# Cross-attention and gated FFN on one core: x of batches 2 to 7 transposed in 32 by 32 blocks on VectorE, scores on sixteen array tiles, a new order for batch 0 and for the periods

## Chip, core and metric

The kernel runs on one core of one Trainium2 chip. The metric is the device time of one execution in microseconds (us). Engines are named as the profile names them: PE is TensorE's matmul queue and PEld its weight loads, DVE is VectorE, ACT ScalarE, POOL GpSimd, SP SyncE, which issues nearly all DMAs.

## What is computed

Per batch (8) and head (8), 512 tokens of x (64 wide) and 32 states are read against each other in both directions; the result, 544 rows of 512 per batch, goes through an RMS norm and a gated FFN with 1536 hidden columns.

```python
B, H, S, Ns, D = (8, 8, 512, 32, 64)
scores = scale * np.matmul(x, state.transpose(0, 1, 3, 2))
a = np.exp(scores - max);  a /= a.sum(-1, keepdims=True) + 1e-09
xread = np.matmul(a, state)                  # tokens read the states
scores2 = scale * np.matmul(state, x.transpose(0, 1, 3, 2))
sread = np.matmul(softmax(scores2), x)       # states read the tokens
x = concatenate([xread, sread], axis=2)      # -> (B*544, 512)
xn = x / sqrt(mean(x * x) + 1e-06) * rms_g
out = (silu(xn @ w_gate) * (xn @ w_val)) @ w_out
```

The three weights come as 64-bit floats, x and state as 32-bit.

## The kernel before

All matmuls are 32-bit; one matmul leaves two MATMUL records in the trace, a transpose leaves one.

The work is a list of **streams**, Python generators whose every `yield` ends one step. Three letter strings, `ORDER`, `PERIOD` and `STATES` (lines 22 to 40), written out by a planner, say which stream takes its next step; within `tc.manual_schedule` they fix the order of the instructions on TensorE, VectorE and ScalarE, each of which takes its queue strictly in that order. GpSimd's and SyncE's queues are ordered by the framework.

- **Batch 0** (`ORDER`, lines 886 to 892). Streams e and d (lines 185 and 208) turn the 64-bit weights into 32-bit ones, 18 pieces of 128 by 1024, the first in two halves: three ScalarE and four VectorE instructions a piece. Meanwhile a (`tokens_read(0)`) and s (`states_read(0)`) do batch 0's attention, A and S batch 1's. v projects a pair of weight blocks onto the states (line 454), h are the hidden products (line 496), t and u their activation, p the output projection (line 694). z (`keep_awake`, line 845) are filler products on TensorE whose results nobody reads.
- **Batches 1 to 7** (`PERIOD`, lines 897 to 920): one period per batch. h, t, u form six pairs of hidden blocks with seven products each (`hidden_seven`, lines 590 to 685; TensorE line 600), 42 steps of h in all; p, c, k project with seven products (`project_seven`, from line 738; TensorE line 754), 14 steps of p. Within period b the streams a and s do the attention of batch b+1, w and v project weights onto states (line 454), x copies them out and lets GpSimd form sums.
- **The states' rows** of all batches come last (`STATES`, lines 921 to 929) in the same seven-product scheme at half width.

**Attention of a batch's tokens** (`tokens_read`, lines 267 to 362): the packed states are transposed on TensorE (272) and copied (275); x, loaded as four chunks of 128 tokens, is transposed on TensorE by 16 transposes (282) in four bursts, each copied by ScalarE (284). Eight products with 64 rows and 32 columns of weights and 512 moving columns (291) give the scores in two PSUM banks. VectorE transposes them in 32 by 32 blocks (302), ScalarE keeps a copy for the states' read (304); maximum, difference, exponential, sum and quotient follow (311 to 327), the transpose back (329), and the read (336: eight products in four row groups, four banks). Squares (343), their sums over four tiles (346), a product with ones (350), the root on GpSimd (254), its spread over the rows (261) and the scaling of `aT_s` (360) end it.

**The states' read** (`states_read`, lines 364 to 411) uses the kept scores: maximum, exponential, eight transposes (385), 32 products (397), one more transpose (408). Line 397 is the last reader of x's buffer; x has two buffers, so the load of batch b+2 can start once batch b's line 397 is done.

SBUF and PSUM come from tile pools: `aps` and `vps` have two PSUM banks each ("at" and "pv"), `fx` two, `fy` and `fz` one. Weights `w_m` have three buffers; each product of line 454 asks for the pair three further on (line 158).

Of the kernel before, what the change touches and what calls it, by code (L numbers as in the profile page):

```python
# [8 lines left out]
F32 = mybir.dt.float32  # L9
# [8 lines left out]
P = 128  # L18
# [4 lines left out]
    "aaaaaaaaddaaaaaaeaseeaasadsasszzzzzzzzzzzzzzssdsaaaasaeadesaeeazzsdasaaezzzzzzza"  # L23
    "deadaaaddeeazzzzsedaadszzzzzadaeedzzvvavdzzadeaAzzzzhdeeddtdAdAAhueheAeedtddphAe"
    "dvdvduvdphedeAedtdhApeehddeuAdddeAhdedvdtudvvpeAAAAdhdAAteAehuhpddephepdeAdAeApA"
    "dteedAAvvveAdpudAAephtdSdhAdphdeAueedhAdeAteudddeeSppAddAAdppAdAdevApvdveehhAdth"
    "AudhpdeddeedeAdteAupvdvdvphedAAtdShhutSAhpukSSSkkkwSwkpSkpwpSSckSScckkpcSwkkkwww"
    "w"
# [3 lines left out]
    "hthtvvhhtuxxhuhthuhththuuhtuuhhxxhhuvxutvhtthuuhuhthuuxhxhxuxtthuhuthhuthuxxhuta"  # L32
    "uahatuhtaxuuuhtauahuahhaahuttuhutauhhhtuuahuhuutauphuauupuauapacasapaaaapapaskaa"
    "aaksacccassppakckpaaackasaapakapaskaaaswpksksswsxxwxxpxcspcskx"
# [4 lines left out]
    "yhuhttyuhuhuuhuthhyuthythytuhuuhuhutuuhuuppcpkpcpukkcpkpkpc"  # L39
# [4 lines left out]
def kernel(  # L44
# [9 lines left out]
):  # L54

# [42 lines left out]
    rows = {}  # L98
    x_sb = {}
# [7 lines left out]

    def load_x(b, *queues):
        x_sb[b] = two.tile([P, NC, H * D], F32, name="x_b")
        for c in range(NC):  # L110
            (queues or (nc.sync,))[c % max(1, len(queues))].dma_start(
                out=x_sb[b][:, c].rearrange("p (h d) -> p h d", h=H),
                in_=x[b, :, P * c:P * c + P, :].rearrange("h p d -> p h d"))
# [153 lines left out]
    def tokens_read(b):  # L267
        xb, packed = x_sb[b], rows.pop(b)
        stT = two.tile([P, 4, Ns], F32, name="stT")
        stT_g[b] = two.tile([P, 4, Ns], F32, name="stT_g")  # L270
# [27 lines left out]
        eS = one.tile([P, 2, S // Ns, Ns], F32, name="eS", tag="eS")  # L298
        m1 = two.tile([P, 2, S // Ns], F32, name="m1")
        z1 = two.tile([P, 2, S // Ns], F32, name="z1")  # L300
# [5 lines left out]

        def along(t, e):
# [13 lines left out]
        for e in range(2):  # L321
            VE.reduce_sum(out=z1[:, e], in_=eS[:, e], axis=AXX)
# [22 lines left out]
        for i, j in ((0, 1), (2, 3), (0, 2)):  # L345
            VE.tensor_tensor(out=sq[:, i, :], in0=sq[:, i, :], in1=sq[:, j, :], op=ALU.add)
            yield
        sp = aps.tile([P, NC], F32, name="at")
# [241 lines left out]
    def hidden_seven(n, weights, tokens, silu, after=lambda mp: None):  # L590
# [67 lines left out]
        def sums():  # L658
            for mp, q in enumerate(pairs):
# [8 lines left out]
                for i, val in ((1, q["c"]), (0, q["x"][:, :, 0:half])):  # L668
# [290 lines left out]
```

## Time and profile before

| what | value |
|---|---|
| median of 3 runs | 800.66 us (800.29 to 801.45) |
| the profiled execution | 800.68 us, span of its instructions 798.9 us |
| TensorE matmul busy | 786.0 us (98%), 4902 records |
| VectorE busy | 515.0 us (64%), 786 instructions |
| ScalarE busy | 347.0 us (43%) |
| GpSimd busy | 179.0 us (22%) |
| DMA | 94.13 MB, 118 GB/s on average |
| chain that ended last | PE 93%, DVE 5% |
| one period, batches 1 to 6 (scores to scores) | 86.90 us |
| line 282 in all | 128 transposes, 0.273 us each as recorded |
| line 845 (filler) | 80 records, 11.2 to 38.2 us |

The span is cut by the program's own structure: batch 0 up to about 141 us, periods of 86.90 us, the states' rows from about 740 us. Times in the views are from the start of the span. A busy share says how full an engine is, not what waits for what; for that the timeline of one engine shows in brackets how long it was idle ahead of an instruction and what released it. A record's own duration contains its pipeline, so the cost of a matmul to the queue is read from start to start.

### The profile page before, as it was taken

The numbers are of one execution on the slowest core, as the hardware profiler recorded it, in microseconds if no ns is written. First come the engines' busy times: TensorE is split into PE (matmuls) and PEld (weight loads), VectorE is DVE, ScalarE is ACT, GpSimd is POOL, SyncE is SP. The second block draws the span as 40 slices with busy tenths as digits, with TensorE's granted clock in tenths as the row PEclk, the third lists the DMA queues.
The fourth block names the chain that finished last, engine by engine and source line by source line (L and its number), as shares of the span: only waits on it lengthen the run. The fifth ranks groups of instructions, "written<-read, shape, count | busy, mean of one in ns | idle before, by whom it ended". The sixth has DMA issues, their size and how long they took to land.

```text
span 798.9 us, 12273 instructions
## 1 busy us (share of the span) xinstructions
PE 786.0 (98%) x4902; PEld 605.2 (76%) x4902; DVE 515.0 (64%) x786; ACT 347.0 (43%) x572; POOL 179.0 (22%) x216
## 2 busy tenths in 40 slices
PE   6999999999999999999999999999999999999998
PEld 5643444788778887888778877888788877888996
DVE  4999996688347842786358833785278635881461
ACT  5998864553245323543255314532354324510320
POOL 0000003530154004510433015500451044400000
PEclk9999999999999999999999999999999999999999
DMA  9987746700182007400461018200540024101311
GB/s 285 262 289 287 263 159 186 264 23 14 34 273 106 1 24 218 185 1 16 127 240 44 4 34 283 107 1 14 193 163 2 14 109 181 66 4 43 113 54 28
DMA packets 61593, 94.13 MB, mean 118 GB/s; under 512 B 38752, under 2 KB 46432, under 8 KB 54624
## 3 DMA queue, kind: packets, MB, share of 16 engines
q1 hardware_dynamic: 59360, 92.75, 34.2%
q10 hardware_dynamic: 2176, 0.59, 0.3%
q8 instruction: 39, 0.64, 0.3%
q14 instruction: 18, 0.15, 0.1%
HBM read 78.12 MB, written 15.20 MB: 117 GB/s over the span
## 4 chain that ended last, share of the span: by engine, by line
PE 93%; DVE 5%; issue 0%; DMA 0%; ACT 0%; SPq 0%
PE f L600 37%; PE f L754 35%; PE f L694 5%; PE pv L496 3%; PE at L454 3%; PE pv L454 3%; PE at L282 2%; PE at L291 1%; DVE ex L232 1%; PE at L397 1%; PE at L336 1%; DVE raw L228 1%; PE at L350 1%; PE at L385 1%; DVE w_m L237 1%
## 5 line engine op out<-in xcount | busy, mean ns | idle before, releaser
L754 PE MATMUL f<-wo,hb 128*128 128x256 f32 x540 | 124.2, 382 | 0.4 <-ACT ot L791 0.2
L662 DVE TENSOR_TENSOR g<-g,f 128x512 f32<-128x512 f32 (+1 forms) x96 | 62.8, 654 | 90.1 <-PE f L600 86.6
L600 PE MATMUL f<-aT_s,v 128*128 128x256 f32 x504 | 119.5, 380 | 0.0
L754 PEld LDWEIGHTS f<-wo,hb 128*128 128x128 f32 x540 | 101.4, 190 | 20.1 <-ACT ot L791 6.9
L600 PEld LDWEIGHTS f<-aT_s,v 128*128 128x128 f32 x504 | 93.8, 190 | 17.3 <-issue 5.2
L254 POOL TENSOR_TENSOR ri<-ss,mhalf 128x4 f32<-128x4 f32 x8 | 9.2, 1156 | 361.8 <-DVE ss L354 361.8
L600 PE MATMUL f<-aT_t,vs 128*128 128x256 f32 x336 | 87.2, 382 | 0.0
L754 PE MATMUL f<-wt,hs 128*128 128x256 f32 x360 | 80.4, 379 | 0.0
L653 ACT ACTIVATE hb<-g 128x1024 f32<-128x1024 f32 (+1 forms) x48 | 48.2, 1004 | 63.0 <-DVE g L662 63.0
L754 PEld LDWEIGHTS f<-wt,hs 128*128 128x128 f32 x360 | 68.3, 190 | 9.5 <-issue 0.2
L791 ACT COPY ot<-f 128x256 f32<-128x256 f32 x60 | 21.5, 372 | 122.5 <-PE f L754 122.5
L600 PEld LDWEIGHTS f<-aT_t,vs 128*128 128x128 f32 x336 | 62.6, 190 | 15.1 <-issue 5.9
L665 DVE SCALAR_TENSOR_TENSOR hb<-hb,g 128x1024 f32<-128x1024 f32 x42 | 55.5, 1320 | 7.8 <-ACT hb L653 7.8
L651 ACT COPY g<-f 128x512 f32<-128x512 f32 (+1 forms) x48 | 26.9, 561 | 76.7 <-PE f L600 76.7
L483 POOL TENSOR_TENSOR vs<-v,vs 128x256 f32<-128x256 f32 x42 | 58.3, 1389 | 0.0
L480 POOL TENSOR_TENSOR vs<-v 128x256 f32<-128x256 f32 x42 | 30.5, 727 | 118.6 <-ACT v L465 118.6
L694 PE MATMUL f<-wo,hb 128*128 128x512 f32 x96 | 44.7, 600 | 0.0
L600 PE MATMUL f<-aT_t,v 128*128 128x256 f32 x168 | 43.9, 383 | 0.0
L496 PE MATMUL pv<-aT_s,v 128*128 128x512 f32 x96 | 43.6, 593 | 0.0
L600 PE MATMUL f<-aT_s,vs 128*128 128x256 f32 x168 | 43.1, 379 | 0.0
L754 PE MATMUL f<-wt,hb 128*128 128x256 f32 x180 | 42.6, 386 | 0.0
L754 PE MATMUL f<-wo,hs 128*128 128x256 f32 x180 | 41.6, 382 | 0.0
(131 smaller groups left out, 1263.4 us busy)
## 6 DMA issues: line engine op xcount, KB each, us to landing
w_m<-w_d SPq DMA_DIRECT2D x48, 1024.0 KB, 6.5
x_b<-in_x_dram SPq DMA_DIRECT2D x30, 256.0 KB, 4.6
out_dram<-ot SPq DMA_DIRECT2D x56, 128.0 KB, 1.8
raw<-in_moe_w_val_dram SPq DMA_DIRECT2D x6, 1024.0 KB, 5.1
raw<-in_moe_w_out_dram SPq DMA_DIRECT2D x6, 1024.0 KB, 7.6
w_d<-w_m SPq DMA_DIRECT2D x6, 1024.0 KB, 4.9
raw<-in_moe_w_gate_dram SPq DMA_DIRECT2D x5, 1024.0 KB, 6.4
raw<-in_moe_w_gate_dram SPq DMA_DIRECT2D x2, 512.0 KB, 4.8
```

The source lines that it names most:

```text
L454: TE.matmul(out=pv[e][Ns * j:Ns * j + Ns, :], lhsT=stT_g[b][D * e:D * e + D, j, :], rhs=w[D * e:D * e + D, j].rearrange("p m k f -> p (m k ...
L480: GE.tensor_tensor(out=vs[:, 0], in0=a21, in1=a22, op=ALU.add)
L483: GE.tensor_tensor(out=vs[:, 2], in0=a12, in1=vs[:, 1], op=ALU.subtract)
L496: TE.matmul(out=to[0], lhsT=lhs(i, k), rhs=r, start=(i == 0), stop=(i == len(rhs) - 1))
L600: TE.matmul(out=ps[:, i, 0:half], lhsT=l[:, i, :], rhs=r, start=(start and i == 0 and k == 0), stop=(k == len(lhs) - 1), skip_group_check= ...
L651: SE.copy(gates(q)[1], q["x"][:, :, 0:half])
L653: SE.activation(out=hb[:, 2 * mp:2 * mp + 2, 0:n].rearrange("p m (c t) -> p m c t", c=2), in_=q["g"][:, :, :, 0:half], func=ACTF.Silu if s ...
L662: VE.tensor_tensor(out=to, in0=to, in1=q[ps][:, :, 0:half], op=ALU.add)
L665: VE.scalar_tensor_tensor(out=h, in0=h, scalar=1.0, op0=ALU.add, op1=ALU.mult, in1=q["g"].rearrange("p m c t -> p m (c t)"))
L694: TE.matmul(out=banks[r], lhsT=hb[:, m, P * r:P * r + P], rhs=wo[:, m, :], start=(m == 0), stop=(m == NM - 1))
L754: TE.matmul(out=banks[name][:, r, :], lhsT=lhs(k)[:, P * r:P * r + P], rhs=rhs(k), start=(start and r == 0 and k == 0), stop=(k == HM - 1) ...
L791: SE.copy(to, banks[name][:, r, :])
```

## The change

**x and scores of batches 2 to 7.** x is loaded by sixteen DMAs of 32 partitions in place of four of 128, so that partition 32g+p of chunk c holds token 128g+32c+p. A new tile `fours` holds all eight heads' states four times, once in each group of 32 partitions, by four DMAs. `scores_of_blocks` transposes `fours` (one VectorE instruction of 128 by 512) and x (two of 128 by 1024) in 32 by 32 blocks; 64 products with 32 rows and 32 columns of weights and 128 moving columns form the scores in four PSUM banks, two of "at" and two of "pv", one for each row group. Their transposes, copies and transposes back are four of 256 columns in place of two of 512. The packed states are still transposed on TensorE, later, straight from PSUM into `stT_g`. Batches 0 and 1 keep the old way (`scores`).

**Batch 0.** Its squares are added by TensorE, sixteen products with ones accumulated in PSUM, in place of three VectorE sums and four products. `ORDER` is new: 31 filler steps in place of 40; batch 0's states' read, all 14 of whose steps stood ahead of the first h, comes late (ten of its steps before the last h, line 397's after it). `slot_sums(1)` moves from the opening of the late pools into the first step of w.

**Periods and states.** `PERIOD` is new: a's first VectorE steps stand after 15, 21 and 24 steps of h, its products of scores after 34; the products of line 336 stand after six steps of p (before: eight); the second pair of v stands after 21 steps of h (before: 15). In `STATES` one p stands ahead of the last h. In `hidden_seven` the first of the two sums of the later pairs comes one step earlier where the activation is Silu (the states' rows).

```diff
--- before.py
+++ after.py
@@ -20,23 +20,22 @@
 W_BUFS = 3
 
 ORDER = (
-    "aaaaaaaaddaaaaaaeaseeaasadsasszzzzzzzzzzzzzzssdsaaaasaeadesaeeazzsdasaaezzzzzzza"
-    "deadaaaddeeazzzzsedaadszzzzzadaeedzzvvavdzzadeaAzzzzhdeeddtdAdAAhueheAeedtddphAe"
-    "dvdvduvdphedeAedtdhApeehddeuAdddeAhdedvdtudvvpeAAAAdhdAAteAehuhpddephepdeAdAeApA"
-    "dteedAAvvveAdpudAAephtdSdhAdphdeAueedhAdeAteudddeeSppAddAAdppAdAdevApvdveehhAdth"
-    "AudhpdeddeedeAdteAupvdvdvphedAAtdShhutSAhpukSSSkkkwSwkpSkpwpSSckSScckkpcSwkkkwww"
-    "w"
+    "aaaaaaaaadaedeeaaaaaaaaaaeeaaaaaaeaeaaazzzzzzzzzzzzzzzzzzzzaeaaaeddddaddzzzzaadd"
+    "deedaaadzvdaeevddzzaeavdedzzzAzhdAeAdtheeheuhAdddAdpetAeduedevvdpvepAhdAedteddde"
+    "hAueheddApdddepvevhdddevdtdupeddeAeehAtshppAAdhduhdedddeeAveeApvdpvdstuededAddeh"
+    "htpddehetpuAddshpvdeuAsedvspAAAAApveshAhAsdtAdudedhedsehtAsAApupdeeAedAppddAdAAv"
+    "AedAvAdpAsvAhSSetdhuShAdhtukkAASwsSkwkkwSpSSSSkpcpSkwskkkckSwpcSSscskwwww"
 )
 
 PERIOD = (
-    "hthtvvhhtuxxhuhthuhththuuhtuuhhxxhhuvxutvhtthuuhuhthuuxhxhxuxtthuhuthhuthuxxhuta"
-    "uahatuhtaxuuuhtauahuahhaahuttuhutauhhhtuuahuhuutauphuauupuauapacasapaaaapapaskaa"
-    "aaksacccassppakckpaaackasaapakapaskaaaswpksksswsxxwxxpxcspcskx"
+    "hhtvvhthhxthxhuhuttuhhthtuuuhhuxuhhxuaxthuthtthuuhhxuutuhtvavhxxtuhxxhtuahuuhhhu"
+    "uxhttuhuhttxhuhhauuuhuthtuatahahtuuuhahhuupuutaauhaauuuuaaaaaaaaaaapapsccaapappa"
+    "ckapcsaukaaasaapacakpaaasksaskkckspsskpspkswwsxwppxxxxsxkscc"
 )
 
 STATES = (
     "hyyyyhthyytthhhuuhtuhththhytuuhuuhthuhhtthyuhyyutyhhhuuuttyuhhutyyhhthuhyhuhuttu"
-    "yhuhttyuhuhuuhuthhyuthythytuhuuhuhutuuhuuppcpkpcpukkcpkpkpc"
+    "yhuhttyuhuhuuhuthhyuthythytuhuuhuhutuuphuupcpkpcpukkcpkpkpc"
 )
 
 
@@ -96,6 +96,7 @@
 
 
     rows = {}
+    fours = {}
     x_sb = {}
 
     def load_state(b):
@@ -105,8 +106,22 @@
             src = state[b, 2 * j:2 * j + 2].rearrange("e n d -> n e d")
             nc.sync.dma_start(out=rows[b][Ns * j:Ns * j + Ns], in_=src)
 
+    def load_fours(b):
+
+        fours[b] = one.tile([P, H, D], F32, name="fours")
+        for g in range(4):
+            nc.sync.dma_start(out=fours[b][Ns * g:Ns * g + Ns],
+                              in_=state[b].rearrange("h n d -> n h d"))
+
     def load_x(b, *queues):
         x_sb[b] = two.tile([P, NC, H * D], F32, name="x_b")
+        if b > 1:
+            for i in range(4 * NC):
+                c, g = divmod(i, 4)
+                nc.sync.dma_start(
+                    out=x_sb[b][Ns * g:Ns * g + Ns, c].rearrange("p (h d) -> p h d", h=H),
+                    in_=x[b, :, P * g + Ns * c:P * g + Ns * c + Ns, :].rearrange("h p d -> p h d"))
+            return
         for c in range(NC):
             (queues or (nc.sync,))[c % max(1, len(queues))].dma_start(
                 out=x_sb[b][:, c].rearrange("p (h d) -> p h d", h=H),
@@ -264,10 +279,10 @@
 
     read = {}
 
-    def tokens_read(b):
-        xb, packed = x_sb[b], rows.pop(b)
+    def scores(b, packed, soft):
+
+        xb = x_sb[b]
         stT = two.tile([P, 4, Ns], F32, name="stT")
-        stT_g[b] = two.tile([P, 4, Ns], F32, name="stT_g")
         tp = aps.tile([P, 4, Ns], F32, name="at")
         TE.transpose(out=tp.rearrange("p j n -> p (j n)"),
                      in_=packed.rearrange("p e d -> p (e d)"), identity=ident)
@@ -295,38 +310,96 @@
 
 
         sS = read[b] = two.tile([P, 2, NC, P], F32, name="sS")
-        eS = one.tile([P, 2, S // Ns, Ns], F32, name="eS", tag="eS")
+        eS = soft["e"] = one.tile([P, 2, S // Ns, Ns], F32, name="eS", tag="eS")
+        for e in range(2):
+            VE.transpose(out=eS[:, e].rearrange("p k n -> p (k n)"), in_=sp[e])
+            yield
+            SE.copy(sS[:, e].rearrange("p c t -> p (c t)"), sp[e])
+            yield "step" if e else None
+
+        soft["st"] = stT
+        soft["half"] = lambda e: eS[:, e]
+        soft["back"] = lambda e: [(aT_s[b][:, e], eS[:, e].rearrange("p k n -> p (k n)"))]
+
+    def scores_of_blocks(b, packed, soft):
+
+        xb = x_sb[b]
+        stB = one.tile([P, H, 2, Ns], F32, name="stB")
+        VE.transpose(out=stB.rearrange("p h k n -> p (h k n)"),
+                     in_=fours.pop(b).rearrange("p h d -> p (h d)"))
+        yield
+
+        xB = one.tile([P, NC, H, 2, Ns], F32, name="xB", tag="xT")
+        for i in range(0, NC, 2):
+            VE.transpose(out=xB[:, i:i + 2].rearrange("p c h k t -> p (c h k t)"),
+                         in_=xb[:, i:i + 2].rearrange("p c f -> p (c f)"))
+            yield
+
+
+        sp = [(aps, vps)[g // 2].tile([P, 2, NC, Ns], F32, name=("at", "pv")[g // 2])
+              for g in range(4)]
+        for e in range(2):
+            for k in range(2):
+                for j in range(4):
+                    for g in range(4):
+                        TE.matmul(out=sp[g][Ns * j:Ns * j + Ns, e].rearrange("n c t -> n (c t)"),
+                                  lhsT=stB[Ns * g:Ns * g + Ns, 2 * j + e, k, :],
+                                  rhs=xB[Ns * g:Ns * g + Ns, :, 2 * j + e, k, :],
+                                  start=(k == 0), stop=(k == 1), skip_group_check=True)
+        yield
+
+
+
+        sS = read[b] = two.tile([P, 2, NC, P], F32, name="sS")
+        eS = one.tile([P, 4, 2, NC, Ns], F32, name="eS", tag="eS")
+        for g in (2, 3, 0, 1):
+            VE.transpose(out=eS[:, g].rearrange("p e c n -> p (e c n)"),
+                         in_=sp[g].rearrange("p e c t -> p (e c t)"))
+            yield
+            SE.copy(sS[:, :, :, Ns * g:Ns * g + Ns], sp[g])
+            yield "step" if g == 1 else None
+        soft["half"] = lambda q: eS[:, 2 * q:2 * q + 2].rearrange("p g e c n -> p (g e c) n")
+        soft["back"] = lambda q: [(aT_s[b][:, :, P * g:P * g + P],
+                                   eS[:, g].rearrange("p e c n -> p e (c n)"))
+                                  for g in (2 * q, 2 * q + 1)]
+
+    def tokens_read(b):
+        packed, soft = rows.pop(b), {}
+        yield from (scores if b < 2 else scores_of_blocks)(b, packed, soft)
+        half = soft["half"]
         m1 = two.tile([P, 2, S // Ns], F32, name="m1")
         z1 = two.tile([P, 2, S // Ns], F32, name="z1")
-        for e in range(2):
-            VE.transpose(out=eS[:, e].rearrange("p k n -> p (k n)"), in_=sp[e])
-            yield
-            SE.copy(sS[:, e].rearrange("p c t -> p (c t)"), sp[e])
-            yield "step" if e else None
 
         def along(t, e):
             return t[:, e].unsqueeze(2).to_broadcast([P, S // Ns, Ns])
 
         for e in range(2):
-            VE.reduce_max(out=m1[:, e], in_=eS[:, e], axis=AXX)
-            yield
-            VE.tensor_tensor(out=eS[:, e], in0=eS[:, e], in1=along(m1, e), op=ALU.subtract)
-            yield
-            SE.activation(out=eS[:, e], in_=eS[:, e], func=ACTF.Exp, scale=SCALE)
+            VE.reduce_max(out=m1[:, e], in_=half(e), axis=AXX)
+            yield
+            VE.tensor_tensor(out=half(e), in0=half(e), in1=along(m1, e), op=ALU.subtract)
+            yield
+            SE.activation(out=half(e), in_=half(e), func=ACTF.Exp, scale=SCALE)
             yield "step"
-        VE.tensor_tensor(out=stT_g[b], in0=stT, in1=rms_g.unsqueeze(2).to_broadcast([P, 4, Ns]),
+        stT_g[b] = two.tile([P, 4, Ns], F32, name="stT_g")
+        if b > 1:
+            soft["st"] = aps.tile([P, 4, Ns], F32, name="at")
+            TE.transpose(out=soft["st"].rearrange("p j n -> p (j n)"),
+                         in_=packed.rearrange("p e d -> p (e d)"), identity=ident)
+            yield
+        VE.tensor_tensor(out=stT_g[b], in0=soft["st"], in1=rms_g.unsqueeze(2).to_broadcast([P, 4, Ns]),
                          op=ALU.mult)
         yield
         aT_s[b] = two.tile([P, 2, S], F32, name="aT_s")
         for e in range(2):
-            VE.reduce_sum(out=z1[:, e], in_=eS[:, e], axis=AXX)
+            VE.reduce_sum(out=z1[:, e], in_=half(e), axis=AXX)
             yield
             VE.tensor_scalar(z1[:, e], z1[:, e], 1e-9, None, op0=ALU.add)
             VE.reciprocal(z1[:, e], z1[:, e])
             yield
-            VE.tensor_tensor(out=eS[:, e], in0=eS[:, e], in1=along(z1, e), op=ALU.mult)
-            yield
-            VE.transpose(out=aT_s[b][:, e], in_=eS[:, e].rearrange("p k n -> p (k n)"))
+            VE.tensor_tensor(out=half(e), in0=half(e), in1=along(z1, e), op=ALU.mult)
+            yield
+            for to, blocks in soft["back"](e):
+                VE.transpose(out=to, in_=blocks)
             yield "step"
 
 
@@ -342,14 +415,18 @@
         for i, j in enumerate((2, 3, 0, 1)):
             SE.activation(out=sq[:, i, :], in_=reads[j], func=ACTF.Square, scale=DM ** -0.5)
             yield "step" if i == 3 else None
-        for i, j in ((0, 1), (2, 3), (0, 2)):
-            VE.tensor_tensor(out=sq[:, i, :], in0=sq[:, i, :], in1=sq[:, j, :], op=ALU.add)
-            yield
+
+        n = 4 if b == 0 else 1
+        if n == 1:
+            for i, j in ((0, 1), (2, 3), (0, 2)):
+                VE.tensor_tensor(out=sq[:, i, :], in0=sq[:, i, :], in1=sq[:, j, :], op=ALU.add)
+                yield
         sp = aps.tile([P, NC], F32, name="at")
-        for c in range(NC):
-            TE.matmul(out=sp[:, c:c + 1], lhsT=sq[:, 0, P * c:P * c + P], rhs=ones,
-                      start=True, stop=True)
-        yield
+        for i in range(n):
+            for c in range(NC):
+                TE.matmul(out=sp[:, c:c + 1], lhsT=sq[:, i, P * c:P * c + P], rhs=ones,
+                          start=(i == 0 and c == 0), stop=(i == n - 1), skip_group_check=True)
+            yield
         ss = two.tile([P, NC], F32, name="ss")
         VE.tensor_scalar(ss, sp, 1e-6, None, op0=ALU.add)
         yield "step"
@@ -665,21 +742,29 @@
                     VE.scalar_tensor_tensor(out=h, in0=h, scalar=1.0, op0=ALU.add, op1=ALU.mult,
                                             in1=q["g"].rearrange("p m c t -> p m (c t)"))
                     yield
-                for i, val in ((1, q["c"]), (0, q["x"][:, :, 0:half])):
+                k = 2 * mp - HM
+                upper, lower = (hb[:, k:k + 2, half * i:half * i + half] if k >= 0 else None
+                                for i in range(2))
+
+                def finish(i, val):
                     part = h[:, :, half * i:half * i + half]
                     if silu:
                         VE.tensor_tensor(out=part, in0=part, in1=val, op=ALU.mult)
                     else:
                         VE.scalar_tensor_tensor(out=part, in0=part, scalar=0.5, in1=val,
                                                 op0=ALU.mult, op1=ALU.mult)
-                    yield
-                if 2 * mp >= HM:
-                    k = 2 * mp - HM
-                    upper, lower = (hb[:, k:k + 2, half * i:half * i + half] for i in range(2))
+
+                def first_sum():
                     VE.tensor_tensor(out=seven["s"][:, k:k + 2, 0:half], in0=lower,
                                      in1=h[:, :, half:n], op=ALU.add)
-                    yield
-                    VE.tensor_tensor(out=lower, in0=upper, in1=lower, op=ALU.subtract)
+
+                steps = [lambda: finish(1, q["c"]), lambda: finish(0, q["x"][:, :, 0:half])]
+                if k >= 0:
+                    steps.insert(1 if silu else 2, first_sum)
+                    steps.append(lambda: VE.tensor_tensor(out=lower, in0=upper, in1=lower,
+                                                          op=ALU.subtract))
+                for step in steps:
+                    step()
                     yield
 
         return products(), copies(), sums()
@@ -847,6 +932,8 @@
             yield
 
     def first_of_batch(b):
+        slot_sums(b)
+        yield
         for mp in range(2):
             for part in own_weights(b, mp):
                 yield from part
@@ -885,10 +972,9 @@
                             mybir.EngineType.Activation})
     with tc.manual_schedule(**by_hand):
         for stream in ORDER:
-            if stream in "ck" and "s" not in seven:
+            if stream in "ckw" and "s" not in seven:
                 early.close()
                 open_late()
-                slot_sums(1)
             next(streams[stream])
     assert all(next(stream, done) is done for name, stream in streams.items() if name != "z")
     load_state(2)
@@ -898,6 +984,8 @@
         if b + 2 < B:
             load_state(b + 2)
             load_x(b + 2)
+        if b + 1 < B:
+            load_fours(b + 1)
         h, t, u = hidden_seven(S, weights_of(b), lambda b=b: tokens_of(b), False)
         p, c, k = project_seven(S, store_tokens(b))
         own = [own_weights(b, mp) for mp in range(2, NM // 2)]
```

More of the change, by code (lines that the diff above doesn't have):

```diff
@@ L297, in tokens_read @@
         sS = read[b] = two.tile([P, 2, NC, P], F32, name="sS")
-        eS = one.tile([P, 2, S // Ns, Ns], F32, name="eS", tag="eS")
-        m1 = two.tile([P, 2, S // Ns], F32, name="m1")
-        z1 = two.tile([P, 2, S // Ns], F32, name="z1")
+        eS = soft["e"] = one.tile([P, 2, S // Ns, Ns], F32, name="eS", tag="eS")
         for e in range(2):
@@ L307, in along @@
+    def tokens_read(b):
+        packed, soft = rows.pop(b), {}
+        yield from (scores if b < 2 else scores_of_blocks)(b, packed, soft)
+        half = soft["half"]
+        m1 = two.tile([P, 2, S // Ns], F32, name="m1")
+        z1 = two.tile([P, 2, S // Ns], F32, name="z1")
         def along(t, e):
@@ L344, in tokens_read @@
             yield "step" if i == 3 else None
-        for i, j in ((0, 1), (2, 3), (0, 2)):
-            VE.tensor_tensor(out=sq[:, i, :], in0=sq[:, i, :], in1=sq[:, j, :], op=ALU.add)
-            yield
-        sp = aps.tile([P, NC], F32, name="at")
-        for c in range(NC):
-            TE.matmul(out=sp[:, c:c + 1], lhsT=sq[:, 0, P * c:P * c + P], rhs=ones,
-                      start=True, stop=True)
-        yield
+        n = 4 if b == 0 else 1
[3 more added lines that the diff above has]
+                yield
+        sp = aps.tile([P, NC], F32, name="at")
+        for i in range(n):
+            for c in range(NC):
+                TE.matmul(out=sp[:, c:c + 1], lhsT=sq[:, i, P * c:P * c + P], rhs=ones,
+                          start=(i == 0 and c == 0), stop=(i == n - 1), skip_group_check=True)
+            yield
         ss = two.tile([P, NC], F32, name="ss")
```

## The prediction

> **What bounds the kernel now.** I first read busy time by stretches of the span, because a share of the whole span averages over two quite different stages.
>
> ```profile
> core 0: us, PE busy (x) PEld busy (x) DVE busy (x) ACT busy (x) POOL busy (x), PEclk, DMA share, GB/s
> 0.00:38.40 38.40, 30.80 (x231) 22.52 (x232) 27.30 (x48) 27.29 (x38) 3.82 (x12) 0.96 0.97 271
> 38.40:141.66 103.26, 102.55 (x479) 43.99 (x478) 91.98 (x115) 75.78 (x95) 9.34 (x12) 1.00 0.70 240
> ...
> 441.38:528.28 86.90, 86.88 (x567) 70.09 (x567) 53.46 (x84) 34.61 (x63) 24.76 (x29) 1.00 0.29 98
> ```
>
> From 38.4 us on TensorE has no hole: 102.55 of 103.26 us in batch 0, 86.88 of 86.90 us in a period of batches 1 to 6. So a microsecond taken off TensorE's queue there is a microsecond off the end, until VectorE (53.5 of 86.9 us) gets in the way. Before 38.4 us TensorE is busy too, but 17 us of that are line 845's filler products; there VectorE and the chain to batch 0's first product (line 496) decide. Second view, TensorE's own timeline: what the removed work costs from start to start.
>
> ```profile
> 253.22 1.03 PE L600 MATMUL f<-aT_t,vs 128*128 128x256 f32 x4
> 254.09 0.60 PE L282 MATMUL at<-ident,x_b 128*128 128x128 f32 x4
> 254.52 1.03 PE L600 MATMUL f<-aT_t,v 128*128 128x256 f32 x4
> ...
> 264.57 1.09 PE L291 MATMUL at<-xT,stT 64*32 64x512 f32 x16
> 265.59 1.99 PE L600 MATMUL f<-aT_s,v 128*128 128x256 f32 x8
> ```
>
> A burst of four transposes of x holds the queue for 254.52 - 254.09 = 0.43 us, the scores for 265.59 - 264.57 = 1.02 us. Third, VectorE's timeline and TensorE's at the start, and TensorE's at the end:
>
> ```profile
> 29.04 1.41 DVE L346 TENSOR_TENSOR sq<-sq 128x512 f32<-128x512 f32 x2
> 36.80 1.22 DVE L360 TENSOR_TENSOR aT_s<-aT_s,at 128x1024 f32<-128x1024 f32 x1 [0.75 <-PE at L261]
> ```
> ```profile
> 38.43 1.88 PE L496 MATMUL pv<-aT_s,v 128*128 128x512 f32 x4
> ...
> 775.88 1.16 PE L600 MATMUL f<-x_t,w_m 128*128 128x128 f32 x8 [0.51 <-DVE c L662]
> ```
>
> The first real product starts 0.4 us after VectorE's line 360 ends; the last hidden product of the states waits 0.51 us for VectorE.
>
> **What the Trainium skill says.** "TensorE: Matmul & The Clock Gate", Part 3, gives a group on sixteen tiles a span of one product and about 4 ns per further tile; its "Wait - 56ns, not 53.3ns?" gives 25 ns as the least distance between starts, however short the product. The trace speaks for the first: line 397 starts 64 short records on four column tiles in 1.03 us, 16 ns each. "TensorEngine Tiling (Array Packing)", Gotcha 1, wants different row tiles in different PSUM banks: line 336 does that with four row groups and four banks, eight products in 1.02 us, and the new scores have four banks as well. "VectorE: DVE Perf Modes", The three transpose paths, says that VectorE transposes 32 by 32 blocks only; the new layout of x is made for that. "DMA: Bandwidth & Descriptors", Rules for kernel authors, says that transfers to disjoint partitions share the same 16 engines: sixteen loads for four win no bandwidth; no run shows such loads of x yet.
>
> **The change, part by part.**
>
> Transposes of x, batches 2 to 7: 16 per batch leave TensorE, 4 x 0.43 = 1.74 us (with rounding) out of a full queue. The state's transpose stays (0.11 us, later). Four ScalarE copies of 0.59 us go; ScalarE is 40% busy, so that is worth nothing.
>
> Scores: 8 products of 512 columns become 64 of 128. A tile now has 4 x 128 = 512 columns, as before, so array time is equal: low end 1.02 us. Records grow from 16 to 128; at line 397's 16 ns that is 2.06 us, at the skill's 25 ns 3.2 us. But line 397's 16 ns is itself array time (64 columns on four tiles), and within one of its rounds starts lie 7 ns apart, which for sixteen tiles is 107 ns, just the time of 128 columns in one record (line 600's record of 256 columns takes 0.216 us). I take 1.1 us. Net per batch -1.74 + 0.08 = -1.66; for six periods **-9.9 us** (ends: -10.4, -4.2 at 16 ns, +2.6 at 25 ns).
>
> VectorE pays. Line 302's transpose of 512 columns takes 0.709 us; rows of 256 and 1024 columns (lines 799, 360) take 0.41 and 1.22. Added: stB 0.71, xB 2 x 1.24, four of 256 for two of 512 twice (+0.34 each), less the stT copy 0.29: +3.6 us per period, 53.5 to 57.1 us of 85.3. What hides it: the three new transposes stand after hidden products 15, 21 and 24, where VectorE idles 0.3 to 1.2 us in a pair's 6 us. What is late next: (1) the projection's third step, which needs hs; it is done at 272.36 and TensorE takes it at 273.46, so 1.1 us of slack; (2) line 336, now asked for after six steps of p instead of eight, 5.2 us earlier, where VectorE was 4.9 us ahead (284.2 against 289.1). I count VectorE's steps in the new order between the last hidden product and line 336 as 11.5 us, against 0.87 + 0.11 + 5 x 2.59 = 13.9 us on TensorE: it fits, with 2.4 us left, if VectorE is not behind already. I take 0.2 us of stall per period, **+1.2 us** (ends: 0 and 1.1 each, +6.6).
>
> Loads: per batch 12 more DMAs of x and 4 of fours on SyncE, at 0.4 to 0.57 us an issue 7 to 8 us of a queue that mostly waits for stores. Weight loads behind them go out later: that for pair 5 is asked for at about 228 us and would leave 8 us later and land 7 us after, at 243; its product, moved from hidden step 15 to 21, is due at about 246. x itself is due most of a period later, fours at hidden step 15, some 12 us after SyncE reaches it. Nothing; if the cover fails, pair 5's product waits 1 to 5 us per period, and VectorE's first attention step with it. The pattern of four PSUM banks takes both banks of pv; the pairs' products that use them are past by then: nothing.
>
> Batch 0: in the new order VectorE has, ahead of line 360, the same 16 conversion steps, but neither the state read's steps (2 x 0.60 + 0.07 + 0.34 + 0.3 + 0.2 = 2.1 us) nor the sums of squares (0.60 + 1.33, 1.9 to 2.0 us). Its queue is full there (27.3 of the 32 us after 6.4), so the first product comes 4.1 us earlier, at 34.3. Twelve more small products of line 350 (3 x 0.95 us) go where filler stood: nothing, since nine fillers fewer are 3.9 us. But batch 0's state read moves into TensorE's full stretch: 8 transposes 0.87, line 397 1.03, one more 0.11 = +2.0 us. Is VectorE in time for the earlier start? Summing its steps up to the conversion of pair 5 gives 34.1 + 74 = 108 us; TensorE gets there at 34.3 + 76 = 110. It is, by a little. Loads of x for batches 2 and 3 move from before 43 us to after 125, when SyncE and the DMA engines have room (0.6 and 0.7 busy in those slices). Sum **-2.1 us**; ends -5 (earlier VectorE also removes TensorE's own small holes) and +2.0 (the first product comes no earlier, the read's cost stays). The slot sums on GpSimd stand right after batch 1's last scaling; 4 x 0.74 us before they are needed some 14 us later: nothing, 3 us if that cover is gone.
>
> States: one step of p (2.59 us) goes ahead of the waiting hidden product and fills the wait: **-0.5 us** (ends 0, -0.5). The sum hs made one step earlier costs nothing, VectorE idles there.
>
> Sum: -9.9 + 1.2 - 2.1 - 0.5 = -11.3. The profiled execution took 800.68 us (span 798.9 and 1.8 around it), the median shown is 800.66: the same. 800.7 - 11.3 = **789.4 us**.
>
> **Rivals.** (a) VectorE is late in each period by the 1.1 us upper end: 789.4 - 1.2 + 6.6 = 794.8. For it: VectorE's work from 253 to 286 us leaves little idle. Against: 30 us of idle per period, and the new steps stand in it. (b) The start brings nothing, so its cost remains: +2.0 for -2.1: 793.5. For it: the start is a chain of ScalarE, VectorE, TensorE and GpSimd, and conversions stand in the way. (c) The change doesn't do what it says: short records on sixteen tiles need 25 ns: 3.2 us for 2.76 before, six times +0.44 for -1.66: 800.7 + 2.6 + 1.2 - 2.1 - 0.5 = 801.9, no change. (d) The slower one: the whole 3.6 us of VectorE's new work arrives at line 336 or at hs; less 1.1 us of slack, 2.5 us of stall in each of six periods, 15.0 instead of 1.2: 803.2. It decides from a lateness of about 3.4 us. For it: line 336 gave up its 4.9 us of lead. Against: two thirds of the work lie before hidden step 25.
>
> **Numbers.** Chances: forecast 0.62 (785 to 793 by itself), (a) 0.17, (b) 0.10, (c) 0.06, (d) 0.05. The range leaves (c) and (d) out, takes in (a) and (b), and goes down to where scores cost 1.02, no stall appears and the start gives 4: 785 to 796. A measurement of this kernel tells 0.2%, 1.6 us, from no change. Faster 0.62 + 0.17 + 0.10 = 0.89; same 0.06; slower 0.05.
>
> **What would show it.** A period of 85.4 us between two batches' scores; scores at 1.0 to 1.2 us from start to start, the new transposes at about 1.24 us and no idle of TensorE at line 336 or at hs; first product of line 496 at 34 us, batch 1's products dense from about 139.5; no 0.5 us wait ahead of the last hidden product. Scores over 1.5 us make the main term wrong; idle of TensorE above 0.5 us per period released by VectorE means (a) or (d); waits for w_m mean that the loads were not hidden.

## The result, and the profile after

The changed kernel takes **833.56 us** (median of 4 runs, 832.0 to 834.51) where the kernel before took 800.89 us beside it (800.29 to 801.45): a ratio of 1.0406, 95% interval 1.0388 to 1.0424. It is 33 us slower, and the forecast was 11 us faster. The profiled execution has a span of 829.9 us (before 798.9).

The same stretches as before, cut in the new kernel at its first hidden product, at batch 1's first hidden products and between the scores of two batches:

```profile
core 0: us, PE busy (x) PEld busy (x) DVE busy (x) ACT busy (x) POOL busy (x), PEclk, DMA share, GB/s
0.00:37.00 37.00, 30.44 (x164) 22.04 (x165) 24.07 (x37) 24.08 (x32) 3.23 (x12) 0.91 0.93 265
37.00:144.84 107.84, 105.81 (x556) 46.54 (x555) 96.76 (x123) 79.00 (x102) 12.36 (x13) 1.00 0.65 229
540.04:632.12 92.08, 88.61 (x663) 72.04 (x662) 55.35 (x90) 32.67 (x60) 23.45 (x29) 0.96 0.22 81
```

A period, from the scores of one batch to those of the next, has become 92.1 us (90.9 in the first two) instead of 86.9. TensorE lacks 3.47 us of it, and its granted clock over the period is 0.96. VectorE is busy for 55.4 us, 1.9 more than before (53.5), so it isn't full. The list of TensorE's waits and the page's clock row and costliest group say where:

```profile
PE f L839 <- DVE ot L884: 21.5, 7, 3.5
```
```profile
PEclk9899999999999999999899989999999989999999
...
L839 PE MATMUL f<-wo,hb 128*128 128x256 f32 x540 | 137.8, 412 | 21.5 <-DVE ot L884 21.5
```

One wait, 3.47 us long in each of six periods (a seventh has the 0.7 us left), holds the projection's products (line 839, 754 before) until VectorE has done an addition of line 884 (799 before). It was on none of the prediction's lists. TensorE's timeline and VectorE's around it:

```profile
574.44 0.60 PE L276 MATMUL at<-ident,ri 128*128 128x128 f32 x4
574.88 0.60 PE L462 MATMUL at<-ident,e 128*128 128x128 f32 x4
578.95 5.49 PE L839 MATMUL f<-wo,hb 128*128 128x256 f32 x12 [3.47 <-DVE ot L884]
584.23 0.90 PE L462 MATMUL at<-ident,e 128*128 128x128 f32 x4
584.97 5.34 PE L839 MATMUL f<-wo,hs 128*128 128x256 f32 x24
```
```profile
572.02 0.41 DVE L884 TENSOR_TENSOR ot<-ot,f 128x256 f32<-128x256 f32 x1
575.08 1.22 DVE L437 TENSOR_TENSOR aT_s<-aT_s,at 128x1024 f32<-128x1024 f32 x1 [2.65 <-PE at L276]
576.22 2.35 DVE L891 TENSOR_TENSOR hs<-hb,hs 128x768 f32<-128x768 f32 x2
578.49 0.41 DVE L884 TENSOR_TENSOR ot<-ot,f 128x256 f32<-128x256 f32 x1
```

The addition at 578.49 is the 7th step of k (k7 below). It reads one half of the PSUM tile "x"; the waiting products, the 10th step of p (p10), write the other half of the same tile. Ahead of it VectorE's queue holds line 437, which itself waits 2.65 us for TensorE's line 276, and two subtractions of line 891. So TensorE waits for a step that stands behind work which TensorE itself released only 3.9 us earlier, when line 276 ended at 575.04. In the kernel before, k7 ran at 297.22, ahead of the scaling (there line 360), and p10 and p11 already stood ahead of it in the order, so that neither waited for it:

```profile
297.22 0.41 DVE L799 TENSOR_TENSOR ot<-ot,f 128x256 f32<-128x256 f32 x1
300.27 1.22 DVE L360 TENSOR_TENSOR aT_s<-aT_s,at 128x1024 f32<-128x1024 f32 x1 [2.65 <-PE at L261]
301.41 0.42 DVE L799 TENSOR_TENSOR ot<-ot,f 128x256 f32<-128x256 f32 x1
```

The diff does it by two orders that changed together. In the old `PERIOD` the 7th k stood behind the 11th p and ahead of the last a, which is the scaling; in the new one (`...kkckspssk...`) it stands ahead of the 10th p and behind the last a. The Trainium skill, "PSUM — Partial Sum Buffer", PSUM bank collisions raise a hardware error, asks a program to guard PSUM by bank and quadrant and not by address, so that one half of a bank is no separate thing to wait for. The trace agrees as far as it goes: p10 begins 0.05 us after k7 ends, though it writes the other half. Whether the two could have overlapped, no run tests.

The second loss is the 5.49 us of those twelve products, 2.76 us at full clock. Stretches before, during and after show the clock:

```profile
568.00:577.95 9.95, 7.48 (x43) 6.51 (x41) 5.04 (x8) 2.74 (x7) 2.51 (x3) 1.00 0.08 26
577.95:584.78 6.83, 5.83 (x15) 4.66 (x16) 1.25 (x3) 0.00 (x0) 2.56 (x3) 0.50 0.07 22
584.78:594.00 9.22, 9.22 (x127) 6.87 (x126) 1.59 (x7) 2.08 (x5) 0.34 (x1) 1.00 0.21 52
```

### The profile page after: what moved, and what is told of

It reads as the page before. It is cut to its first block, busy times and chain, and to the rows that moved or that the text cites. A ratio compares the mean times of both kernels' runs of the same rounds, so it can differ in the third digit from the quotient of the medians.

```text
span 829.9 us, 13595 instructions
## 1 busy us (share of the span) xinstructions
PE 795.9 (96%) x5484; PEld 615.8 (74%) x5484; DVE 528.5 (64%) x819; ACT 335.4 (40%) x560; POOL 170.6 (21%) x216
## 4 chain that ended last, share of the span: by engine, by line
PE 92%; DVE 4%; DMA 2%; SPq 1%; issue 1%; ACT 0%; DVEq 0%
PE f L839 35%; PE f L677 33%; PE pv L573 5%; PE f L779 4%; PE at L531 3%; PE pv L531 2%; PE f L930 2%; DVE hs L891 2%; PE at L427 1%; SPq L121 1%; PE at L409 1%; DVE wt L820 1%; PE at L345 1%; PE at L474 1%; DMA w_m<-w_d 1%
## 5 line engine op out<-in xcount | busy, mean ns | idle before, releaser
L839 PE MATMUL f<-wo,hb 128*128 128x256 f32 x540 | 137.8, 412 | 21.5 <-DVE ot L884 21.5
L839 PEld LDWEIGHTS f<-wo,hb 128*128 128x128 f32 x540 | 109.7, 207 | 39.9 <-DVE ot L884 23.2
L557 POOL TENSOR_TENSOR vs<-v 128x256 f32<-128x256 f32 x42 | 33.5, 797 | 184.4 <-ACT v L542 184.4
L884 DVE TENSOR_TENSOR ot<-ot,f 128x256 f32<-128x256 f32 x45 | 18.5, 416 | 79.8 <-PE f L839 77.0
L542 ACT COPY v<-pv 128x512 f32<-128x512 f32 x42 | 23.4, 589 | 48.7 <-PE pv L531 47.8
L839 PE MATMUL f<-wt,hb 128*128 128x256 f32 x180 | 40.8, 382 | 0.0
```

The source lines that it names most:

```text
L542: SE.copy(v[:, e].rearrange("p m k f -> p (m k f)"), pv[e])
L557: GE.tensor_tensor(out=vs[:, 0], in0=a21, in1=a22, op=ALU.add)
L839: TE.matmul(out=banks[name][:, r, :], lhsT=lhs(k)[:, P * r:P * r + P], rhs=rhs(k), start=(start and r == 0 and k == 0), stop=(k == HM - 1) ...
```

## The experiments

**1. The k step alone, put back behind p's 10th.** Theory A is the above; theory B is that VectorE's 3.6 us of new work is what arrives late, wherever it stands.

```
-    "ckapcsaukaaasaapacakpaaasksaskkckspsskpspkswwsxwppxxxxsxkscc"
+    "ckapcsaukaaasaapacakpaaasksaskkcspksskpspkswwsxwppxxxxsxkscc"
```

> One letter of the period's order moves: the first of the two additions on the x bank (the seventh step of k) is written behind the tenth step of p in place of ahead of it. Theory 1 (a wait written into the order): TensorE's tenth step of p waits 3.5 us in each of six periods only because a VectorE read of its PSUM tile was written ahead of it, and the 6.8 us of half clock that follow come from that wait; both go: a period of 85.9 to 86.2 us in place of 90.9 to 92.1, total 796 to 799 us. Theory 2 (VectorE is late with its 3.6 us of new work): the wait reappears at the next consumer, the eleventh step of p, which needs hs: 2 us or more of idle per period there, total above 810 us.

Measured: 793.74 us (792.68 to 794.87), ratio to before 0.991 (0.9896 to 0.9925). A period, TensorE and VectorE of this kernel:

```profile
432.00:517.48 85.48, 85.48 (x679) 69.93 (x675) 56.09 (x90) 32.74 (x61) 23.47 (x29) 1.00 0.32 103
```
```profile
551.30 0.60 PE L462 MATMUL at<-ident,e 128*128 128x128 f32 x4
551.74 2.76 PE L839 MATMUL f<-wo,hb 128*128 128x256 f32 x12
554.33 0.60 PE L462 MATMUL at<-ident,e 128*128 128x128 f32 x4
```
```profile
552.64 2.35 DVE L891 TENSOR_TENSOR hs<-hb,hs 128x768 f32<-128x768 f32 x2
554.92 0.74 DVE L884 TENSOR_TENSOR ot<-ot,f 128x256 f32<-128x256 f32 x2
```

The addition comes as late as in the changed kernel, 2.3 us after line 891 begins, and nobody waits for it. TensorE has no hole in the period and keeps the full clock. In this order of the rest, one step's place costs 833.56 - 793.74 = 39.8 us. VectorE's new work is all there; theory B falls.

**2. The same wait cut at its other end:** k7 stays ahead of p10, and line 437's scaling moves behind it, so that k7 no longer stands behind that.

```
-    "ckapcsaukaaasaapacakpaaasksaskkckspsskpspkswwsxwppxxxxsxkscc"
+    "ckapcsaukaaasaapacakpaaasksskkckaspsskpspkswwsxwppxxxxsxkscc"
```

> On VectorE the scaling of aT_s, which waits for GpSimd's root and its spread by TensorE, moves behind the seventh step of k; the order of k against p stays as in the changed kernel. Theory 1: the read of the x bank is late only because this scaling stands ahead of it; VectorE then reaches it when the ninth step of p ends, TensorE waits under 0.5 us, full clock stays: period 85.9 to 86.4 us, total 796 to 800 us. Theory 2: VectorE is late by its sum of work, whatever the order: the wait stays above 2 us, total above 815 us.

Measured: 795.55 us (794.89 to 796.52), ratio 0.9933 (0.9916 to 0.9949), period 85.79 us. With line 437 out of the way k7 may stand ahead of p10: it is the pair of orders that costs, not one of them. The third way, a bank for each half of the tile, was not tried.

**3. Filler in the wait.** If the clock falls because TensorE is idle, then eight products nobody reads, put into the hole, bring the clock back and leave the wait where it is.

```
+    def fill_wait():
+        ps = vps.tile([P, 2, P], F32, name="pv")
+        for i in range(8):
+            TE.matmul(out=ps, lhsT=ident, rhs=ident.unsqueeze(1).to_broadcast([P, 2, P]),
+                      start=True, stop=True)
+        yield
...
-    "ckapcsaukaaasaapacakpaaasksaskkckspsskpspkswwsxwppxxxxsxkscc"
+    "ckapcsaukaaasaapacakpaaasksaskkcksqpsskpspkswwsxwppxxxxsxkscc"
```

> Eight filler products of the kind of batch 0 (about 3.5 us, into a bank of pv that is free there) go ahead of the tenth step of p in each of the six periods; nobody reads them. Theory 1: the half clock after the wait comes from TensorE's idleness; with the wait filled the tenth step takes 2.6 us in place of 4.3 to 5.5 and the period 88.5 to 89.5 us, total 815 to 820 us. Theory 2: the long tenth step has another cause (shared PSUM or SBUF access); the total stays at 832 us or rises by the filler's excess.

Measured: 816.12 us (a single run), period 89.2 us. TensorE's timeline of this kernel:

```profile
565.06 0.60 PE L462 MATMUL at<-ident,e 128*128 128x128 f32 x4
565.50 3.62 PE L938 MATMUL pv<-ident 128*128 128x256 f32 x16
569.13 2.86 PE L839 MATMUL f<-wo,hb 128*128 128x256 f32 x12
```

Useless work fills the hole, and p10 is back at normal length. So the 39.8 us split: 833.56 - 816.12 = 17.4 us are the clock (15.9 against the changed kernel's profiled execution, 832.0), 816.12 - 793.74 = 22.4 us the wait, 3.7 in each of six periods. The records agree: from p10 to p11 the changed kernel takes 6.02 us (578.95 to 584.97), experiment 1 takes 3.03. Over the six periods of the profiled execution that is 15.2 us, 1.6 and 1.8 in the first two periods and 2.8 to 3.0 in the other four.

**4. The new start alone:** old `PERIOD`, scores and loads of x for every batch; new `ORDER`, squares by TensorE, late slot sums and new `STATES`.

```
-        if b > 1:
+        if b > B:
...
-        yield from (scores if b < 2 else scores_of_blocks)(b, packed, soft)
+        yield from (scores if b < B else scores_of_blocks)(b, packed, soft)
```

> Batches 2 to 7 keep the old loads of x, TensorE's transposes, the old scores and the old period order; only batch 0's new order, its squares added by TensorE, the moved slot sums and the states' order are in. As predicted: -2.1 and -0.5 us, 798 us. By the two traces, in which batch 1's products become dense 2.3 us later after the change: +2.3 -0.5, 802 to 803.5 us.

Measured: 800.81 us (799.63 to 802.38), ratio 1.0003 (0.9994 to 1.0011). No difference. Its first hidden product and two waits of TensorE later in batch 0:

```profile
35.23 1.88 PE L573 MATMUL pv<-aT_s,v 128*128 128x512 f32 x4
...
126.40 0.63 PE L462 MATMUL at<-ident,e 128*128 128x128 f32 x4 [0.91 <-DVE aT_s L437]
136.62 0.41 PE L485 MATMUL at<-ident,sr 128*128 128x128 f32 x2 [1.05 <-DVE sr L481]
```

The first product comes 3.2 us earlier than before (38.43), and batch 1's first hidden products 0.5 us later (143.02 for 142.55). These 3.2 us and the 0.5 us went to batch 0's state read (2.0 us by the prediction's own count) and to the two waits, 1.96 us together.

**5. The order of the scores' products,** the loops over g and j exchanged, on top of experiment 1: do neighbours in the queue disturb each other?

```
-                for j in range(4):
-                    for g in range(4):
+                for g in range(4):
+                    for j in range(4):
```

> On the version with the k step moved. The 64 products of scores run with the column tile innermost, so four products in turn go to one row group; measured with the row group innermost: 1.83 us from start to start, 16.6 ns a product once the first sixteen are through. Theory A (loads of weights and products of one row group exclude each other, whatever the order): the same, 1.7 to 1.95 us. Theory B (the order of row groups decides the overlap): four in turn in one row group overlap less, over 2.3 us, or more, under 1.4 us.

Measured: 792.65 us (a single run), scores 1.84 us, period 85.48. The order makes no difference. (The 16.6 ns of the expectation are about those of a record; a product leaves two.)

**6. Each of the 64 products of the scores cut in two of 64 columns,** on top of experiment 1. If columns cost, 128 halves take the same 1.83 us; if products cost, twice that.

```
+                for c in (0, 2):
                     ...
-                                   rhs=xB[Ns * g:Ns * g + Ns, :, 2 * j + e, k, :],
+                                   rhs=xB[Ns * g:Ns * g + Ns, c:c + 2, 2 * j + e, k, :],
```

> On the version with the k step moved. Each product of scores is split into two of 64 moving columns, 128 products for 64, same result. If the 1.83 us were the array's time for the moving columns, it stays near 1.8 to 2.0 us; if it is a cost per product (weight load or issue), it goes to 3.0 to 3.7 us; half and half (a load of 32 columns and the moving columns in turn in each row group) gives 2.4 to 2.8 us.

Measured: 811.98 us (a single run). The scores take 3.30 to 5.20 us from start to start in the six periods, each with one hole in it. Less its hole each takes 2.8 to 3.0 us: about 23 ns for a product of half the columns, against 1.83 us / 64 = 28.6 ns. Half of the columns save only 6 ns, so about 17 of the 28.6 ns (an estimate from these two figures) belong to the product, whatever its columns; the result lies between the expectation's "half and half" and its "cost per product". One hole is 0.39 us long, the other five 1.7 to 2.3 us, and nothing in the trace releases them (the line has four of them):

```profile
PE pv L346 <- issue: 7.7, 4, 2.3
```

Why TensorE stops there stays open.

**7. The start of before with the new periods** (experiment 1, with the old `ORDER`, VectorE's sums of squares and the slot sums at the pools' opening).

```
-        n = 4 if b == 0 else 1
+        n = 1
...
-        slot_sums(b)
-        yield
...
+                slot_sums(1)
```

> The version with the k step moved, with batch 0 as in the kernel before: old order, three VectorE sums of squares, slot sums where the late pools open. New loads of x, VectorE's transposes, the scores on sixteen tiles and the mended period stay. By the run of the start alone (no difference to before): 793 to 795 us, the same as with the new start. By the prediction's term for the start (-2.1 us): 795.8 us or more.

Measured: 791.71 us (790.84 to 791.94), ratio to before 0.9888 (0.9872 to 0.9905), the shortest time of all. The gain is 800.77 - 791.71 = 9.06 us: six periods of 86.90 - 85.48 = 1.42 us, which is 8.5, and 0.5 us, the hole that the states' rows had.

**8. The two waits of experiment 4 mended** in the new order, on top of experiment 1: the last two steps of A, with batch 1's scaling, go ahead of two k, and the scaling of batch 1's state read (line 481, a step of S) goes straight behind that read's products.

```
-    "AedAvAdpAsvAhSSetdhuShAdhtukkAASwsSkwkkwSpSSSSkpcpSkwskkkckSwpcSSscskwwww"
+    "AedAvAdpAsvAhSSetdhuShAdhtuAAkkSwsSkwkkwSpSSSSkpcpSSkwskkkckwpcSSscskwwww"
```

> The version with the k step moved; in batch 0's order two steps of the weight sums go behind batch 1's scaling of aT_s, and the scaling of batch 1's state read goes straight behind its products. If the start's gain is lost in the two waits of 0.9 and 1.05 us of TensorE near 127 and 138 us, both shrink and the total falls by 1 to 2 us, to 792 us; if the start is held by VectorE's sum of work, the waits move and the total stays at 793.7 us.

Measured: 792.03 us (791.13 to 793.08), ratio 0.9892 (0.9877 to 0.9906). Both waits are gone from the trace, and 793.74 - 792.03 = 1.7 us with them, of the 2.0 us that they took (the runs of the two kernels still overlap, at 792.68 to 793.08). That brings the new start level with the old one (791.71), not ahead of it.

## Why the prediction was wrong

**The failed step is the stall of VectorE, "What is late next".** It took 0.2 us of stall per period, 6.6 us at most in all, from a list of two places: the third step of p that needs hs, and line 336. TensorE waits for VectorE at neither of them in any run. The wait came at a third place, p10 behind k7: 3.47 us in each of six periods, 22.4 us by experiment 3. The prediction followed what each moved step of a, v and p needs. It never asked where k, which only drains results, stands against p. The diff shows k7 ahead of p10 there and the scaling ahead of k7, and the profile of before had most of the price: 2.65 us of waiting ahead of line 360, its own 1.22 us, and line 806's two subtractions (0.95 us each), which the new order puts behind the scaling. They take 2.35 us there, beside GpSimd's line 595.

**The clock had no term.** Every cost was counted at full speed. In the periods 3.47 us of idleness cost another 1.6 to 3.0 us by half clock, 17.4 us in all by experiment 3. The prediction's own view of the start held the warning: its first stretch has a mean clock of 0.96. The Trainium skill ("TensorE: Matmul & The Clock Gate", Part 1, What's actually happening) gives the mechanism, a free-running window of about 3.4 us after whose idleness the clock is halved. The lengths of 3.41 and 6.83 us, one window and two, agree with it, and all changes of the clock in this trace lie on one grid of 3.41 us. No window without any work was needed: TensorE was busy for 0.3 to 1.2 us of each of the six windows after which the clock fell.

**Rival (d)** had the right sign, but the wrong mechanism and place: all of VectorE's new work arriving at line 336 or hs, for 803.2 us, still 30 short of what was measured. Experiment 1 keeps that work (VectorE is busy 2.6 us more in a period than before) and is 7 us faster than before. By the prediction's own figures more than two thirds of it stand ahead of hidden step 25, 0.71 + 2 x 1.24 = 3.19 of 3.6 us. The sign that the prediction named, idle of TensorE above 0.5 us per period released by VectorE, appeared, and pointed to the wrong suspects.

**Right: the transposes.** Four bursts of 0.44 us left TensorE's queue, 1.75 us per period by the sums from start to start (predicted 1.74).

**Right mechanism, wrong size: the scores.** They take 1.83 us, not 1.1, above the estimate but below the 2.06 us that 16 ns a record gave. By the prediction's own sign, scores over 1.5 us, its main term was wrong. TensorE's records of the changed kernel:

```profile
538.22 1.89 PE L677 MATMUL f<-aT_s,v 128*128 128x256 f32 x8
540.04 0.30 PE L345 MATMUL at<-xB,stB 32*32 32x128 f32 x2
...
540.36 0.41 PE L345 MATMUL at<-xB,stB 32*32 32x128 f32 x3
...
541.87 1.13 PE L677 MATMUL f<-aT_s,v 128*128 128x256 f32 x4
```

The first sixteen products, one on each tile, start within 0.32 us, 20 ns apart; the other 48 need 1.51 us, 31 ns each. The prediction took the pace of a first round for that of four. The term is +0.81 per period in place of +0.08.

**Not foreseen, in the other direction:** fewer changes between kinds of products. In experiment 1's period lines 677, 839 and 462 together take 0.48 us less than lines 600, 754 and 385 did before, with the same products, and TensorE's queue changes from one line to another 24 times instead of 35; that the changes are the cause is argued from the sums, not tried alone. So -1.75 + 0.81 - 0.48 = -1.42, which is what the period of experiment 1 measures. The prediction had -1.66 + 0.2 = -1.46: near only by luck, since the scores' error of 0.73 us is cancelled by this 0.48 us and by a stall of 0.2 us that doesn't appear there.

**The start** came out as in rival (b), no gain, though its first product did come earlier: by 1.4 us in the changed kernel and 3.2 in experiment 4, not 4.1. VectorE's sums were gone, but TensorE took their place. The prediction put the twelve more products with ones at nothing; the sixteen hold the queue for 3.99 us (25.30 to 29.29), where four held it for 0.89 before. While they run, the clock falls to half:

```profile
25.06:28.47 3.41, 3.41 (x31) 3.18 (x29) 3.38 (x4) 3.38 (x5) 0.00 (x0) 1.00 0.53 132
28.47:31.88 3.41, 3.41 (x23) 1.52 (x23) 3.34 (x6) 2.73 (x3) 1.39 (x1) 0.50 0.88 339
```
```profile
25.30 4.13 PE L427 MATMUL at<-ones,sq 128*128 128x1 f32 x32
...
30.42 1.96 PE L531 MATMUL at<-w_m,stT_g 64*32 64x512 f32 x16
...
34.18 1.06 PE L276 MATMUL at<-ident,ri 128*128 128x128 f32 x4
```
```profile
29.89 1.39 POOL L269 TENSOR_TENSOR ri<-ss,mhalf 128x4 f32<-128x4 f32 x1 [27.49 <-DVE ss L431]
```

GpSimd's root is ready at 31.28, but TensorE's queue comes to its spread, line 276, only at 34.18, behind line 531 and filler at half clock; VectorE's line 437 waits 1.21 us for it. The four transposes of line 276 hold the queue 0.85 us instead of 0.44 there. All eight profiled kernels with the new start have half clock for 6.83 us here, and in all eight TensorE's records fill the 3.41 us ahead of it without a gap. With the old start it was 3.41 us (the profile of before, behind a gap of 0.99 us) and none (experiment 7). So a queue that is full by its records can lose the clock too. That products with a single column don't hold it is what these traces suggest; no run changed those products alone. And the count of VectorE's total work up to pair 5 was no test of the two waits near 127 and 138 us, which are again a matter of who stands ahead of whom (experiment 8).

**The loads** are hidden in the periods, as said. Once, in front of batch 2, they are not. The queue of SyncE and TensorE's line behind it:

```profile
141.07 15.11 SPq L121 DMA_DIRECT2D x_b<-in_x_dram  x27
156.28 7.02 SPq L167 DMA_DIRECT2D w_m<-w_d  x4
```
```profile
161.79 1.09 PE L531 MATMUL at<-w_m,stT_g 64*32 64x512 f32 x16 [0.23 <-DMA w_m<-w_d]
```

Twenty-seven loads of x hold the queue for 15 us, and the weights behind them arrive 0.2 us late (0.4 to 1.1 us in experiments 1 to 3, 5 and 8).

**The states** gained their 0.5 us: the last hidden product starts at 809.60 directly behind p, without a wait.

With the k step moved, the forecast change comes to 793.74 us, inside the prediction's range of 785 to 796, and partly by luck: the gain is 7.4 us instead of 11.3, because the start gives nothing, and the periods come out right by errors that cancel. The kernel as written has one dependence more that the sum does not contain.

## What to carry to other kernels

In an order written out by hand, go through every PSUM tile and list who reads it and who writes it next, in each engine's queue. Then ask what stands ahead of the reader: its lateness is that of the whole queue before it, not its own 0.4 us. A hole of 3.5 us in TensorE has to be priced with the half clock after it, here another 1.6 to 3.0 us, and a few filler products tell the two apart. Where work moves to TensorE, mind its granted clock there too, and not only whether its queue is full.

## What was unexpected in the hardware

- An idleness of 3.47 us brought half clock for 3.41 us in two periods and for 6.83 us in four. In this trace the place of the wait on the grid of 3.41 us goes with it. In the two short cases TensorE was busy for 3.06 and 3.41 us of the first window at half clock; in the four long ones for 2.2 to 2.5 us, and full clock came only after the next window, which was full. The four runs of the changed kernel have mean clocks of 0.975 and 0.971, which fits four long cases and six (half of 4 x 6.83 + 2 x 3.41 or of 6 x 6.83 us, and of the start's 6.83), so the mix differs from run to run. Here is one case of each kind in the columns of the first view, the window of the wait and the one after it:

```profile
301.54:304.95 3.41, 0.92 (x4) 0.84 (x5) 2.44 (x3) 0.00 (x0) 3.33 (x4) 1.00 0.03 9
304.95:308.36 3.41, 3.41 (x9) 2.58 (x9) 0.00 (x0) 0.00 (x0) 0.64 (x1) 0.50 0.09 29
482.44:485.85 3.41, 0.98 (x9) 0.74 (x7) 2.83 (x3) 0.96 (x2) 1.45 (x2) 1.00 0.00 0
485.85:489.26 3.41, 2.37 (x6) 1.92 (x7) 0.99 (x2) 0.00 (x0) 2.60 (x3) 0.50 0.11 38
```

- Sixteen tiles with products of 32 by 32 by 128 columns did not keep the pace of their first round (20 ns a product), only 31 ns in the later ones, in either order of the loops.
- VectorE and GpSimd hold each other up, and the one that begins second pays. The first of line 891's two subtractions takes 0.95 us, as in the kernel before; GpSimd's line 595, which begins 0.16 us after it, takes 1.37 us instead of 0.72. The second subtraction begins while line 595 runs and takes 1.48 us (the two are one line of 2.35 us above); line 596 begins while that one runs and takes 1.32.

```profile
576.38 1.37 POOL L595 TENSOR_TENSOR aT_t<-aT_s 128x256 f32<-128x256 f32 x1 [3.17 <-DVE aT_s L437]
577.83 1.32 POOL L596 TENSOR_TENSOR aT_t<-aT_s,aT_t 128x256 f32<-128x256 f32 x1
579.11 0.72 POOL L598 TENSOR_TENSOR aT_s<-aT_s 128x256 f32<-128x256 f32 x1
```
